# Attention and mixture of experts on one core: expert 5's first layer in pairs of chunks, its list work kept out of the pairs, and two PSUM banks for the last lists

## The chip, the cores and the metric

One core of a Trainium2 chip runs the whole program. The metric is device time in microseconds (us), lower is better. The time of the kernel before is the median of three runs.

## The reference, cut to what matters

An attention over channels makes a 256-wide row for each of 20224 tokens. A gate then assigns each token to one of 8 experts, at most 2528 tokens each, greedily by logit; expert e computes `relu(x @ w1[e]) @ w2[e]` for its tokens.

```
for e in range(8):                       # w1[e]: 256 x 1024, w2[e]: 1024 x 256
    mask = assigned == e
    h = np.maximum(x[mask] @ w1[e], 0.0)
    out[mask] = h @ w2[e]
```

## The kernel before, in words

The attention comes first and takes about the first third of the span. The rest is the experts, numbered p = 0 to 7 in the order in which they are processed. An expert has 2528 rows in 20 columns of 128 (the last has 96), worked on in five chunks of four columns: chunk (p, c) is 512 rows, the last 480.

Every float32 operand is split into a high and a low part, and three products (high by high, low by high, high by low) are summed. So **layer1** takes, for each of 8 blocks of 128 hidden columns, two halves of the contraction by three products: 6 matmuls of 512 columns, 48 for a chunk. TensorE writes `ph` tiles (four PSUM banks, ring of 4); ScalarE writes `hH` (relu, line 1581), VectorE the rest `hL` (line 1586). **layer2** takes 24 matmuls of 256 columns for each of 20 columns into `py` (two banks); ScalarE copies out `y` (line 1628), and GpSimd scatters it to its tokens (line 1630).

For the experts in `PARTED` the chunks (1, 2) and (3, 4) go through **layers** instead: a two-by-two block product with seven products for eight (a Winograd form), over halves of the contraction and halves of the hidden columns, and over the two chunks. For four groups the seven products of three matmuls are issued in the order written out in `STEPS`: 84 matmuls of 512 columns for a pair. It needs sums of weight quarters (**sums_w**, lines 1328 to 1335, spread over the end of the expert before) and of the rows (**turn_parts**, lines 1437 to 1446), and the results are joined with VectorE and ScalarE (lines 1666 to 1686). For an expert outside `PARTED` weights are split by **split_w** (line 1298) and rows by **turn** (lines 1509 to 1516). An expert in `PARTED` loads its second weight into the same buffer as its first, so it asks for it only at the end of the expert before (`load_w`, `LOAD_AT`).

Which tokens an expert gets is found beside the experts' own matmuls, as streams of small steps. **route(p)** searches a threshold (VectorE and ScalarE count, a tiny matmul adds over partitions); **compact(p)** makes the list: a running count, then 20 tests of 128 list places, three to a group. A group is three matmuls into `pi` (line 1022), three ScalarE sign passes with an accumulator (line 1079) and one copy `ext` (line 1082); then some fifteen small VectorE steps. In the kernel before all groups of lists 1 to 7 use one bank, so a group's matmuls follow the copy of the group before.

The order of all engines' instructions is fixed when the program is built, by the class **Order**: it keeps a modelled TensorE time `pe` and VectorE time `dve`; `tick` adds a matmul's time and calls `hook`, which issues whatever is due, the main work (splits, sums, `hL`) ahead of the streams at equal time. A step "P" of a stream goes to TensorE only when its input should have been ready for `margin` (700 ns); "p" goes at once; "A" is a ScalarE step. `want` holds a load back until its list is done.

```
elif eng in "Pp":
    if eng == "p" or st.ready + self.margin <= self.pe:
        self.pe += cost
        st.mine = st.ready = self.pe + PE_TO_DVE
```

Rows of a chunk are gathered by GpSimd (line 1392) and moved twice by SP's queue. `turn(5, 0)` asks for chunk (5, 2); `turn_parts(p, c)` for an even c asks for the two chunks behind it.

Of the kernel before, what the change touches and what calls it, by code (L numbers as in the profile page):

```python
# [8 lines left out]
F32 = mybir.dt.float32  # L9
# [12 lines left out]
E, F = 8, 1024  # L22
# [7 lines left out]
NCOL = -(-CAP // 128)  # L30
LASTC = CAP - (NCOL - 1) * 128
GW = C + E
RB = 3
# [55 lines left out]
SLACK = 450  # L89
DEPTH = 4  # L90
PAD_X = 88
PARTED = (6, 7)
LOAD_AT = (1, 0)
STEPS = (
# [8 lines left out]
def attention_moe(ctx: ExitStack, tc: tile.TileContext, q, k, vt, tau, wg, w1t, w2t, tabs, out):  # L103
# [3 lines left out]
    P = nc.gpsimd  # L107
# [884 lines left out]
    def compact(p):  # L992
# [27 lines left out]
        def tested(pi, g0, n):  # L1020
            for i in range(n):
                PE.matmul(pi[:, i * W:(i + 1) * W], lhsT=G[:, (g0 + i) * 128:(g0 + i + 1) * 128], rhs=E_,  # L1022
                          start=True, stop=True)
# [40 lines left out]
        if p == 0:  # L1064
# [3 lines left out]
                yield "W", 0  # L1068
            yield ve(NCOL)
            V.tensor_scalar(at[:, 0:NACT], sgn[:, 0:NACT], 0.5, COLS / 2.0, op0=OP.mult, op1=OP.add)  # L1070
        for g0 in range(0, NCOL if p else 0, RB):
            n = min(RB, NCOL - g0)
            pi = ps_c.tile([128, 512], F32, name="pi")
            yield "P", n * 75
            tested(pi, g0, n)
            for i in range(n):
                yield "A", 600
                junk = rtile("junk", dt=BF, bufs=2)
                S.activation(junk, pi[:, i * W:i * W + COLS], AF.Sign, bias=rhalf[:, g0 + i:g0 + i + 1], scale=-1.0,
                             accum_out=sgn[:, g0 + i:g0 + i + 1])  # L1080
            yield "A", 200
            S.activation(ext[:, g0:g0 + n], pi[:, 0:n * W].rearrange("p (i w) -> p i w", w=W)[:, :, COLS:W], AF.Copy)
        if p:
            yield ve(NCOL)
            V.tensor_scalar(at, sgn, 0.5, COLS / 2.0, op0=OP.mult, op1=OP.add)
# [59 lines left out]
    class Order:  # L1145
        def __init__(self):
            self.pe = self.dve = 0.0
            self.margin = 0
            self.patient = False
            self.main = []  # L1150
            self.streams = []

# [18 lines left out]
        def hook(self):  # L1171
            moved = True
            while moved:
                moved = False
                best = None
                if self.main:
                    best = (max(self.dve, self.main[0][0]) + self.patient * GAP, 0, None)
                for st in list(self.streams):
                    if st.next is None:
                        self.streams.remove(st)  # L1180
                        continue
                    eng, cost = st.next
                    if eng == "W":
                        st.step()
                        if st.next is None or st.next[0] != "W":
                            moved = True
                            break
                    elif eng == "M":
                        st.mine = max(st.mine, cost)
                        st.step()  # L1190
                        moved = True
                        break
                    elif eng == "A":
                        if st.ready <= self.pe:
                            st.mine = st.ready = self.pe + cost + ACT_LAT
                            st.step()
                            moved = True
                            break
# [4 lines that stand above are left out]
                            st.step()  # L1203
                            moved = True
                            break
                    else:
                        c = (max(self.dve, st.mine) if eng == "V" else self.dve, st.prio(), st)
                        if self.patient and c[1] == EARLY_PRIO:
                            c = (c[0] + EARLY_GAP,) + c[1:]
                        if best is None or c[:2] < best[:2]:  # L1210
                            best = c
                if moved:
                    continue
                if best is not None and best[0] <= self.pe + SLACK:
                    moved = True
                    if best[2] is None:
                        self.run_main()
                    else:
                        st = best[2]
                        self.dve = best[0] + st.next[1]  # L1220
                        st.mine = self.dve + DVE_TO_DVE
                        st.ready = self.dve + DVE_TO_PE
                        st.step()
            plan()
# [12 lines left out]
    o = Order()  # L1237
# [163 lines left out]
    def gather():  # L1401
        for _ in range(2 if queue and queue[0][1] == 0 else 1):
            if queue:
                queue.pop(0)[2]()
# [234 lines left out]
    def layers(p, c):  # L1639
        o.flush(turned[0])  # L1640
        w = parts_w[p]
        (aH, aL), (bH, bL) = xts[p, c], xts[p, c + 1]
        sH, sL = own["s"]
        x = {"11": (aH[:, 0], aL[:, 0]), "12": (aH[:, 1], aL[:, 1]), "s3": (bH[:, 0], bL[:, 0]),
             "22": (bH[:, 1], bL[:, 1])}
        for i, name in enumerate(("s1", "s2", "s4")):
            x[name] = sH[:, i], sL[:, i]
        while queue:
            gather()
        h = [[ffx.tile([128, 8, 512], F32R, name=name) for name in ("hH", "hL")] for _ in range(2)]  # L1650
        seeded = [(ph_tile(), len(phs) - 1) for _ in range(4)]
        fresh = [ps_2.tile([128, 512], F32, name="py") for _ in range(2)]
        sums = {}
        kept = {}

        def product(dst, a, b, g, first=False):
            n = 0
            f = slice(g * 128, (g + 1) * 128)
            for i, l in ((0, 0), (0, 1), (1, 0)):
                PE.matmul(dst, lhsT=w[b][l][:, f], rhs=x[a][i], start=(first and n == 0), stop=(n == 2),  # L1660
                          skip_group_check=True)
                n += 1
                o.tick(227)

        def copy(dst, src):
            S.activation(dst, src, AF.Copy)

        def joined(key, dst, src):
            V.tensor_tensor(dst, src, kept["p7"], op=OP.add)
            sums[key] = dst  # L1670
            o.dve += 690

        for step in STEPS:
            op, g = step.split(".")
            g = int(g)
            A, D = fresh[g % 2], fresh[1 - g % 2]
            Bk, Z = seeded[g % 2][0], seeded[2 + g % 2][0]
            if op[0] in "hl":
                place = {"11": (0, g, A), "12": (0, 4 + g, Z), "21": (1, g, sums.get(("21", g))),
                         "22": (1, 4 + g, sums.get(("22", g)))}  # L1680
                t, f, src = place[op[2:]]
                hH, hL = h[t]
                if op[0] == "h":
                    S.activation(hH[:, f], src, AF.Relu)
                else:
                    V.scalar_tensor_tensor(hL[:, f], src, 0.0, hH[:, f].bitcast(F32), op0=OP.max, op1=OP.subtract)
                    o.dve += 690
            elif op == "cAB":
                copy(Bk, A)
            elif op == "cBZ":  # L1690
                copy(Z, Bk)
            elif op == "p7":
                kept["p7"] = ffx.tile([128, 512], F32, name="p7", bufs=1)
                copy(kept["p7"], D)
            elif op == "j22":
                sums["22", g] = ffx.tile([128, 512], F32, name="c22", bufs=1)
                joined(("22", g), sums["22", g], Z)
            elif op == "j21":
                joined(("21", g), Bk, Bk)
            else:  # L1700
                {"P1": lambda: product(A, "11", "11", g, True), "P7": lambda: product(D, "s3", "t3", g, True),
                 "P6": lambda: product(Bk, "s2", "t2", g), "P2": lambda: product(A, "12", "21", g),
                 "P5": lambda: product(Z, "s1", "t1", g), "P4": lambda: product(Bk, "22", "t4", g),
                 "P3": lambda: product(Z, "s4", "22", g)}[op]()
                settle()
                gather()
        unit[0] += 1
        for _, at in seeded:
            phs[at] = unit[0]
        lows[p, c] = lows[p, c + 1] = unit[0]  # L1710
        return h
# [207 lines left out]
```

## Time and profile before

| what | value |
|---|---|
| median of 3 runs | 1247.6 us (1247.07 to 1250.76) |
| profiled execution | 1246.64 us, of which the span is 1244.6 us |
| granted TensorE clock | 1.0 of full speed throughout |
| TensorE matmul busy | 1228.4 us, 99% of the span |
| VectorE, ScalarE, GpSimd busy | 902.8, 630.9, 386.5 us |

The span is the time from the first to the last instruction of the profiled execution; the execution has 2.04 us around it. Matmul records overlap, so the busy time of TensorE is an upper view of its work; its start times show the pace.

### The profile page before, as it was taken

What the parts mean: (1) busy time and instruction counts of PE and PEld (TensorE: products, weight loads), DVE (VectorE), ACT (ScalarE), POOL (GpSimd) and SP (SyncE); (2) the same over time, 40 slices, a digit from 0 to 9 for tenths busy, and PEclk for the clock granted to TensorE, in tenths of its full rate; (3) what the DMA queues carried; (4) which work ended last, traced back from release to release, by engine and by line L of the source; (5) the groups of instructions that cost most, each with busy time, mean ns of one, the idle gap of its engine ahead of it and who ended that gap; (6) DMA issues with size and microseconds to landing.
All of it is one profiled execution on the core that took longest, in us unless ns stands there. A gap on an engine that the chain in (4) does not pass through costs nothing.

```text
span 1244.6 us, 23776 instructions
## 1 busy us (share of the span) xinstructions
PE 1228.4 (99%) x8734; PEld 1100.3 (88%) x8734; DVE 902.8 (73%) x2574; ACT 630.9 (51%) x1491; POOL 386.5 (31%) x693
## 2 busy tenths in 40 slices
PE   8999999999999999999999999999999999999998
PEld 7888977899888988998999899988988998989898
DVE  6688587798778777867867888887775455756752
ACT  6646653367233543524533655547555544554652
POOL 1000000001442263244443443541453344344422
PEclk9999999999999999999999999999999999999999
DMA  9999876236233054255432633362544335554510
GB/s 314 314 405 415 327 241 217 119 155 236 69 85 104 33 124 134 53 131 117 140 81 73 176 93 99 79 171 55 128 120 105 80 88 148 114 119 114 116 37 33
DMA packets 222516, 179.37 MB, mean 144 GB/s; under 512 B 152384, under 2 KB 193216, under 8 KB 217792
## 3 DMA queue, kind: packets, MB, share of 16 engines
q1 hardware_dynamic: 195328, 98.41, 29.0%
q0 software_dynamic: 17664, 58.22, 14.6%
q10 hardware_dynamic: 9408, 21.24, 4.4%
q8 instruction: 68, 1.11, 0.4%
q14 instruction: 48, 0.39, 0.1%
HBM read 118.06 MB, written 59.77 MB: 143 GB/s over the span
## 4 chain that ended last, share of the span: by engine, by line
PE 81%; issue 7%; DVE 4%; DMA 3%; POOL 3%; ACT 2%; SPq 0%; POOLq 0%; ACTq 0%; DVEq 0%
PE py L1623 30%; PE ph L1578 27%; PE px L285 8%; PE s L337 7%; DMA x_d<-xs 2%; PE pc L811 2%; POOL out_dram L1630 2%; PE ph L1660 2%; PE py L1660 1%; PE px L459 1%; PE pi L1022 1%; DVE acc_q L351 1%; POOL xg L1392 1%; DMA ua<-in_q_dram 1%; DVE acc_k L351 1%
## 5 line engine op out<-in xcount | busy, mean ns | idle before, releaser
L1623 PE MATMUL py<-uc,hH 128*128 128x256 f32 (+1 forms) x2560 | 336.8, 280 | 0.4 <-ACT c L1628 0.3
L1623 PEld LDWEIGHTS py<-uc,hH 128*128 128x128 f32 (+1 forms) x2560 | 314.1, 187 | 2.9 <-ACT c L1628 0.5
L1578 PE MATMUL ph<-xH,ua 128*128 128x512 f32 (+3 forms) x1056 | 285.0, 387 | 0.1
L1586 DVE SCALAR_TENSOR_TENSOR hL<-ph,hH 128x512 fp32r<-128x512 f32 (+3 forms) x264 | 175.6, 666 | 83.1 <-ACT hH L1581 79.9
L1581 ACT ACTIVATE hH<-ph 128x512 fp32r<-128x512 f32 (+3 forms) x264 | 152.7, 579 | 155.9 <-PE ph L1578 149.6
L1578 PEld LDWEIGHTS ph<-xH,ua 128*128 128x128 f32 x1056 | 189.9, 188 | 33.9 <-ACT xH L1542 0.4
L1630 POOL DMA_INDIRECT out_dram<-y,idx x104 | 107.5, 1034 | 325.0 <-ACT y L1628 297.7
L1623 PE MATMUL py<-uc,hL 128*128 128x256 f32 (+1 forms) x1280 | 179.3, 280 | 0.0
L1392 POOL DMA_INDIRECT xg<-x_d,src x156 | 156.2, 1001 | 67.0 <-issue 56.0
L1578 PE MATMUL ph<-xL,ua 128*128 128x512 f32 (+3 forms) x528 | 161.5, 385 | 0.0
L1623 PEld LDWEIGHTS py<-uc,hL 128*128 128x128 f32 (+1 forms) x1280 | 161.0, 187 | 0.2
L1628 ACT ACTIVATE y<-py 128x256 f32<-128x256 f32 (+1 forms) x104 | 39.7, 381 | 151.6 <-PE py L1623 137.9
L1578 PEld LDWEIGHTS ph<-xL,ua 128*128 128x128 f32 x528 | 97.3, 188 | 17.8
L337 PE MATMUL s<-ua 128*128 128x256 f32 x320 | 73.7, 387 | 2.0 <-DMA ua<-in_k_dram 1.5
L288 ACT ACTIVATE xs<-px 128x512 f32<-128x512 f32 (+2 forms) x98 | 49.7, 519 | 47.2 <-PE px L285 45.4
L337 PEld LDWEIGHTS s<-ua 128*128 128x128 f32 x320 | 61.1, 194 | 13.5 <-issue 3.0
L337 PE MATMUL s<-uc 128*128 128x256 f32 x320 | 71.3, 380 | 0.0
L337 PEld LDWEIGHTS s<-uc 128*128 128x128 f32 x320 | 60.3, 190 | 8.8 <-issue 0.8
L285 PE MATMUL px<-aH,vh 128*128 128x256 f32 (+1 forms) x232 | 67.8, 294 | 0.3 <-ACT vh L261 0.3
L285 PE MATMUL px<-aH,vl 128*128 128x256 f32 (+1 forms) x232 | 65.9, 284 | 1.5 <-DVE vl L264 1.5
L1630 POOL DMA_INDIRECT out_dram<-c,idx x30 | 29.4, 981 | 120.4 <-ACT c L1628 109.9
L285 PE MATMUL px<-aL,vh 128*128 128x256 f32 (+1 forms) x232 | 65.9, 285 | 0.0
(432 smaller groups left out, 1977.5 us busy)
## 6 DMA issues: line engine op xcount, KB each, us to landing
x_d<-xs ACTq DMA_DIRECT2D x39, 512.0 KB, 2.7
xr<-xg SPq DMA_DIRECT2D x34, 512.0 KB, 3.3
xq<-xr SPq DMA_DIRECT2D x136, 128.0 KB, 3.7
vr<-in_vt_dram SPq DMA_DIRECT2D x14, 1024.0 KB, 9.9
uc<-in_k_dram SPq DMA_DIRECT2D x18, 512.0 KB, 6.3
uc<-in_q_dram SPq DMA_DIRECT2D x18, 512.0 KB, 8.2
ua<-in_k_dram SPq DMA_DIRECT2D x17, 512.0 KB, 6.5
ua<-in_q_dram SPq DMA_DIRECT2D x17, 512.0 KB, 7.8
```

Source lines behind the costliest of these rows:

```text
L285: mm = PE.matmul(px[:, i * C:i * C + width], lhsT=l_, rhs=a_, start=(j == 0), stop=(j == len(terms) - 1))
L288: S.activation(xs[:, t % TH:t % TH + n, 0:width], px[:, 0:n * width].rearrange("p (t c) -> p t c", t=n), AF.Copy)
L337: newest[0] = PE.matmul(sb[:, ib * C:(ib + 1) * C], lhsT=kt[:, t, ib * 128:(ib + 1) * 128], rhs=qt[:, t, :], start=(first and t == 0 and i ...
L351: V.tensor_tensor(acc, acc, sq, op=OP.add)
L1392: P.indirect_dma_start(out=xg[:n, i, :], out_offset=None, in_=x_d, in_offset=bass.IndirectOffsetOnAxis(ap=at, axis=0))
L1578: PE.matmul(ph[:, 0:nt], lhsT=l[:, w], rhs=x_[:, kb, 0:nt], start=(i == 0), stop=(i == 5))
L1581: S.activation(hH[:, fb, 0:nt], ph[:, 0:nt], AF.Relu)
L1586: V.scalar_tensor_tensor(hL[:, fb, 0:nt], ph[:, 0:nt], 0.0, hH[:, fb, 0:nt].bitcast(F32), op0=OP.max, op1=OP.subtract)
L1623: PE.matmul(py[:n, 0:C], lhsT=l[:, fb, tk], rhs=w[:, d], start=(j == 0), stop=(j == 23))
L1628: S.activation(y[:n], py[:n, 0:C], AF.Copy)
L1630: sd = P.indirect_dma_start(out=out, out_offset=bass.IndirectOffsetOnAxis(ap=idx[:n, col:col + 1], axis=0), in_=y[:n], in_offset=None)
L1660: PE.matmul(dst, lhsT=w[b][l][:, f], rhs=x[a][i], start=(first and n == 0), stop=(n == 2), skip_group_check=True)
```

## The change

`PARTED` becomes (5, 6, 7): the two chunk pairs of expert 5 go through `layers`, with everything that belongs to it (sums of weights at the end of expert 4, sums of rows, the late load of the second weight). While the products of a pair are issued, the streams rest (`o.held`). For the lists of experts 6 and 7 the groups of tests alternate between the bank `pi` and the bank `pc`, and a group's matmuls are issued as "p", after the second sign pass of the group before it, in place of "P" after that group's copy.

```diff
-PARTED = (6, 7)
+PARTED = (5, 6, 7)
...
-        for g0 in range(0, NCOL if p else 0, RB):
-            n = min(RB, NCOL - g0)
-            pi = ps_c.tile([128, 512], F32, name="pi")
-            yield "P", n * 75
-            tested(pi, g0, n)
+        banks = 2 if p >= E - 2 else 1
+
+        def counted(g0, n, kind):
+            pool, name = (pcnt, "pc") if banks == 2 and g0 // RB % 2 else (ps_c, "pi")
+            pi = pool.tile([128, 512], F32, name=name)
+            yield kind, n * 75
+            tested(pi, g0, n)
+            held.append((pi, g0, n))
+        held = []
+        groups = [(g0, min(RB, NCOL - g0)) for g0 in range(0, NCOL if p else 0, RB)]
+        for g in groups[:1 if p else 0]:
+            yield from counted(*g, "P")
+        for at_ in range(len(groups)):
+            pi, g0, n = held.pop(0)
             for i in range(n):
                 yield "A", 600
...
+                if banks == 2 and at_ + 1 < len(groups) and i == min(1, n - 1):
+                    yield from counted(*groups[at_ + 1], "p")
             yield "A", 200
...
+            if banks == 1 and at_ + 1 < len(groups):
+                yield from counted(*groups[at_ + 1], "P")
...
-                for st in list(self.streams):
+                for st in () if self.held else list(self.streams):
...
+        o.held = True
         for step in STEPS:
...
+        o.held = False
```

## Rows read from the trace of the kernel before

**Rows 1.** The page, part 1: busy time of each engine over the span.
```profile
PE 1228.4 (99%) x8734; PEld 1100.3 (88%) x8734; DVE 902.8 (73%) x2574; ACT 630.9 (51%) x1491; POOL 386.5 (31%) x693
```

**Rows 2.** Stretches of experts 5, 6, 7: length, PE, PEld, DVE, ACT, POOL busy, clock.
```profile
916.22:1029.45 113.23, 113.23 (x766) 101.65 (x765) 58.23 (x126) 58.69 (x175) 45.71 (x84) 1.00 0.43 103
1029.45:1135.30 105.85, 105.44 (x699) 95.28 (x697) 68.33 (x110) 57.38 (x112) 46.89 (x86) 1.00 0.52 129
1135.30:1240.20 104.90, 104.83 (x698) 94.90 (x696) 56.61 (x91) 52.18 (x101) 32.33 (x61) 1.00 0.28 69
```

**Rows 3.** Timeline of TensorE, layer 1 of expert 5: start us, us, operation.
```profile
919.15 1.07 PE L1578 MATMUL ph<-xH,ua 128*128 128x512 f32 x4
920.51 0.38 PE L1022 MATMUL pi<-E__106,G 128*128 128x162 bf16 x3
922.15 1.07 PE L1578 MATMUL ph<-xH,ua 128*128 128x512 f32 x4
...
948.35 0.31 PE L1022 MATMUL pi<-E__106,G 128*128 128x162 bf16 x2
```

**Rows 4.** Timeline of TensorE: a 480-row chunk's ends, a pair's ends.
```profile
997.28 1.03 PE L1578 MATMUL ph<-xH,ua 128*128 128x480 f32 x4
1007.67 1.08 PE L1623 MATMUL py<-uc,hH 128*128 128x256 f32 x8
...
1052.12 0.64 PE L1660 MATMUL py<-xH,ua 128*128 128x512 f32 x2
...
1071.49 0.64 PE L1623 MATMUL py<-uc,hH 128*128 128x256 f32 x4
```

**Rows 5.** VectorE's groups by line in expert 6: count, busy us, mean ns, idle before.
```profile
L1443 DVE TENSOR_TENSOR xg<-xg 128x512 f32<-128x512 f32 x8 | 5.5, 692 | 0.3
```

**Rows 6.** Stretches around the starts of expert 5 and expert 6, columns likewise.
```profile
904.00:916.00 12.00, 12.00 (x107) 11.96 (x106) 10.45 (x37) 3.49 (x8) 5.71 (x12) 1.00 0.17 59
916.00:928.00 12.00, 12.00 (x61) 9.49 (x60) 9.93 (x22) 8.69 (x25) 9.03 (x17) 1.00 0.47 134
928.00:940.00 12.00, 12.00 (x62) 9.54 (x61) 5.57 (x9) 8.07 (x27) 0.00 (x0) 1.00 0.81 196
1040.00:1052.00 12.00, 11.74 (x99) 11.34 (x97) 10.24 (x16) 5.23 (x11) 4.46 (x7) 1.00 0.48 133
```

**Rows 7.** Timelines of GpSimd, ScalarE, VectorE, TensorE, start of expert 6.
```profile
1028.66 0.95 POOL L1286 DMA_INDIRECT ub<-in_w2t_dram,ei  x1 [0.30 <-issue]
...
1035.62 0.63 ACT L1295 ACTIVATE uc<-ub 128x512 fp32r<-128x512 f32 x1 [2.59 <-DMA ub<-in_w2t_dram,ei]
...
1036.89 0.68 DVE L1586 SCALAR_TENSOR_TENSOR hL<-ph,hH 128x512 fp32r<-128x512 f32 x1
...
1043.36 1.31 DVE L1437 STREAM_TRANSPOSE xg<-xq 128x512 f32<-128x512 f32 x2 [0.24 <-issue]
...
1048.94 0.69 DVE L1443 TENSOR_TENSOR xL<-xg,xH 128x512 fp32r<-128x512 f32 x1
...
1037.67 1.15 PE L1578 MATMUL ph<-xH,ua 128*128 128x512 f32 x4
...
1049.29 1.18 PE L1623 MATMUL py<-uc,hH 128*128 128x256 f32 x8 [0.26 <-ACT c L1628]
```

**Rows 8.** Timeline of VectorE: list 6, from its head to its index.
```profile
915.32 0.16 DVE L998 CAST cb<-sc_a 128x1 bf16<-128x1 f32 x1
...
954.19 0.17 DVE L1128 SCALAR_TENSOR_TENSOR idx<-bt,src 128x20 int32<-128x20 f32 x1
```

**Rows 9.** ScalarE's groups by line in expert 5, and TensorE's wait in list 5.
```profile
L1079 ACT ACTIVATE junk<-pi,rhalf 128x160 bf16<-128x160 f32 x40 | 15.4, 391 | 3.3 <-PE pi L1022 3.0
L1079 ACT ACTIVATION_READ_ACCUMULATOR junk<-pi,rhalf 128x1 f32 x40 | 8.1, 203 | 0.0
L1082 ACT ACTIVATE ext<-pi 128x6 f32<-128x6 f32 (+1 forms) x14 | 2.5, 178 | 0.0
...
842.92 0.37 PE L1022 MATMUL pi<-E__106,G 128*128 128x162 bf16 x3 [1.42 <-ACT ext L1082]
```

More of the change, by code (lines that the diff above doesn't have):

```diff
@@ L1149, in __init__ @@
             self.patient = False
+            self.held = False
             self.main = []
```

## The prediction, made before the changed kernel ran

> **What bounds the kernel now.** I read the page first, then the stretches of the last experts, then TensorE's timeline inside them, and last the other engines where work is added. The page shows TensorE's matmuls busy for 99% of the span, VectorE for 73%, ScalarE for 51% [rows 1]. Overlapping records make the 99% an upper view, so I checked the timeline: in expert 5 matmuls follow each other at a steady pace with no idle time in the stretch, at clock 1.00 [rows 2]. What counts here is therefore the number of matmuls, and any wait that a late VectorE or ScalarE forces on TensorE. Expert 5 takes 113.23 us, expert 6, which has its pairs already, 105.85, and expert 7 104.90 [rows 2]. The second step is to see how much of the difference is pairs and how much is list work, because both lists 6 and 7 are made inside expert 5.
>
> **List work on TensorE.** Six matmuls of a block take 920.51 − 919.15 = 1.36 us; with a group of list tests ahead of them 922.15 − 920.51 = 1.64 [rows 3]. A group costs 0.28 us. Lists 6 and 7 have 14 groups, and each list a head of two small matmuls that I price alike: 16 × 0.28 = 4.5 us. They are still 14 groups after the change, so this cost moves but does not shrink.
>
> **The pairs, what they save.** I price it three ways.
> - Count: three 512-row chunks of 8 × 1.36 = 10.88 us and one 480-row chunk of 1007.67 − 997.28 = 10.39 [rows 3, 4] make 43.03. Two pairs of 1071.49 − 1052.12 = 19.37 [rows 4] make 38.74. Saved: 4.29 us.
> - Expert 5 without list work, 113.23 − 4.5 = 108.73, against expert 6's 105.85 [rows 2]: 2.9.
> - The same against expert 7's 104.90 [rows 2]: 3.8.
>
> The second holds expert 6's own small waits and the third has no next expert to prepare, so the gross gain lies between 2.9 and 4.3. I take 3.7.
>
> A pair has 12 matmuls fewer than two chunks, at 1.36 / 6 = 0.227 us each [rows 3]. The Trainium skill, "TensorE: Matmul & The Clock Gate", section "Back-to-back issue gap", gives about 131 ns for a sustained 512-column matmul beside its weight load. By it the 24 matmuls saved would be worth an estimated 3.1 us; the trace's pace in this kernel is 0.227, and I go by that.
>
> **What the pairs add on VectorE, and where.** The weight sums at the end of expert 4 are 11 VectorE instructions (seven low parts, four differences) where `split_w` had 4: seven more. The turn of chunk (5, 2) has four mixed sums and three more low parts: seven more again. At 0.69 us [rows 5] each lot is 4.8 us. The joins inside the pairs have room: those of expert 6 fit, and the streams rest there. The two lots fall between 896 and 940 us, in expert 4's last stage and expert 5's first. There VectorE is busy 10.45, 9.93 and 5.57 of three times 12 us [rows 6], so 10.05 us are idle and 9.6 are to be added, while threshold 6 is still being finished: list 6 has its head at 915.32 [rows 8]. Main work goes first at equal time, so what is late first is the list: I expect its head 3 to 6 us later, its first tests at about 925 to 930.
>
> **The wait at expert 5's start.** The start of expert 6 shows what a first expert in pairs does without list work. The second weight's load is issued at 1028.66, behind the four gathers of the next chunk; ScalarE waits 2.59 us for it with the relu copies queued behind, VectorE's low part for the third block comes at 1036.89, TensorE's seventh block needs it at 1037.67 and is a trace slower, the row sums start only at 1043.36, and a `py` bank comes free 0.26 us late at 1049.29 [rows 7]. There was no slack to speak of, and no list. In the changed kernel the same transition comes at 916, with the same load position (`LOAD_AT` is chosen by expert 4, which is not paired), and 3 to 5 us of threshold and list instructions stand in VectorE's order between its low parts. VectorE cannot pass them while it waits behind ScalarE. Bounds: if they all run in time that VectorE idles anyway the extra wait is nothing; if all 9.6 us of added work end up late, 3.2 us of it are still covered (the low part that expert 6's second product reads was done at 1048.94 + 0.69 = 1049.6 [rows 7], and that product comes three matmuls after 1052.12 [rows 4], at 1052.8), and 6.4 us reach TensorE. The nearest row is the start of expert 6, whose 0.26 us lies near the low end; I take a quarter of the way up, 1.7.
>
> **The streams at rest.** List 6 in the kernel before goes from 915.32 to 954.19 [rows 8], groups 4.64 us apart (948.35 − 920.51 over 6) [rows 3]. In the changed kernel the first pair stands at about 916 + 11 + 11 = 938 and rests the streams for 19.4 us; the second pair stands at about 979. List 6 is wanted by `turn_parts(5, 4)` at about 968, and its gathers run beside the products of the second pair. List 7 has the whole of expert 6. So the rest costs nothing as long as list 6 ends by about 979; the price beyond is the third rival. Below nothing I see no gain: in experts 6 and 7 no stream runs in the pairs before either.
>
> **Two banks.** A group needs 3 × (391 + 203) + 178 ns = 1.96 us of ScalarE [rows 9], so 4.64 us a group was not ScalarE's limit. By the planner's own costs (3 × 720 + 320 ns, rounded up to its ticks) I estimate 3.2 us a group, 7 × 3.2 = 22 us for a list. That is what lets list 6 end before 979: two or three groups by 938, the rest from 957 to about 973, some 3 us of small steps. A group's matmuls now wait for a copy two groups back, which the order issues about 1.3 us ahead of them, as far as before. Such a wait did reach TensorE once, 1.42 us in list 5 when ScalarE was behind [rows 9]. Bounds are nothing and one such wait for each list, 2.8; I take 0, since ScalarE is below 75% in these stretches [rows 6].
>
> **The sum.** 3.7 − 1.7 = 2.0 us less than the profiled execution's 1246.64: 1244.6. That execution lies 0.96 below the median of the runs shown, 1247.6, so I forecast 1245.6.
>
> **Rivals.**
> - No new wait: the transition hides as it does for expert 6. Gain 3.7 to 4.3, time 1243.3 to 1243.9. For it: TensorE lost only 0.4 us in all of expert 6 [rows 2]. Against it: that start was at its limit without a list. Chance 0.20.
> - VectorE is the bound between 896 and 940. The 10.05 us idle [rows 6] are mostly waits for ScalarE's copies, and can be filled only in part. If half can be used, 9.6 − 5.0 = 4.6 us are late; if none, 9.6, less the 3.2 covered, and some 1.5 at the end of expert 5's first chunk. TensorE waits 3 to 8 us, the time is 1247 to 1252. It decides against the change from a wait of 3.7 us up. Chance 0.17.
> - List 6 misses the second pair, and rests there until about 998. Its last steps and the gathers of chunk (6, 0) then come 20 us later, with 10 to 15 us to landing and turn (1028.4 to 1043.36 for the same chain [rows 7]); expert 6 would wait up to 5 us on top of 1.7: 1246 to 1251. Chance 0.08.
> - Gathers held up by VectorE. The changed turns and sums read two SBUF operands where the old ones read PSUM, and if such an instruction kept GpSimd out of SBUF, four gathers might each be 0.69 us late [rows 5], the rows of (5, 2) 2.8 us: 1248.4. GpSimd's instructions say no: 46.89 / 86 = 0.545 us each in expert 6, 45.71 / 84 = 0.544 in expert 5 [rows 2]. Chance 0.03. The Trainium skill, "SBUF — State Buffer", section "Who interferes with whom", has this rule for GpSimd instructions that read SBUF; the trace does not bear it out for the time of GpSimd's instructions here.
>
> **How the numbers follow.** The forecast, a gain of 0.4 to 3.7 us, has 0.52, its own range 1243.9 to 1247.2. The range takes in the first rival and most of the second: from 1242.9 (0.4 below the first rival, as medians differ by about that) to 1249.6; about 0.15 is left out. A change of 0.3%, 3.7 us, is about what a measurement of this kernel can tell from none. Faster by more: nearly all of the first rival, 0.18. Slower by more: a quarter of the second, half of the third and some of the fourth, and what I have not seen, 0.12. Within: 0.70.
>
> **What would show it.** Expert 5 about 111 us long for 113.23, with 168 matmuls in its two pairs and one chunk of 48 left; list groups about 3.2 us apart and none inside a pair; ScalarE waiting 2 to 3 us for the second weight at about 919; idle time of TensorE between 919 and 940, in sum 1 to 3 us, put down to VectorE or ScalarE; expert 6 as long as before. It is wrong if that idle time is over 4 us or nothing, if list 6's index lies behind 979, or if TensorE waits at `pi` or `pc`.

## The result, and the profile after

The changed kernel takes 1258.19 us (median of 4 runs, 1257.49 to 1258.33), the kernel before beside it 1247.34. The ratio over the runs is 1.0083, 95% interval 1.0071 to 1.0095: slower, by 10.85 us between the medians, where 1245.6 and "no change that can be told" had the most chance. The profiled execution took 1257.49 us, 10.85 above that of before as well.

The stretches of experts 5, 6 and 7, cut where layer 1 of each begins, with the columns of [rows 2]:

```profile
916.96:1041.56 124.60, 114.16 (x744) 103.18 (x742) 79.11 (x172) 73.81 (x206) 47.60 (x86) 0.96 0.44 110
1041.56:1146.48 104.92, 104.77 (x698) 94.93 (x697) 69.59 (x117) 57.87 (x112) 44.81 (x82) 1.00 0.48 119
1146.48:1251.05 104.57, 104.57 (x698) 94.79 (x696) 56.39 (x91) 52.25 (x101) 32.73 (x61) 1.00 0.28 69
```

Expert 5 takes 124.60 for 113.23 [rows 2], 11.4 us more, and it holds the loss: it starts only 0.7 us later than before, and experts 6 and 7 are 0.9 and 0.3 shorter. Its 24 matmuls fewer (22 by the records, of which a few can be missing) did not help, for TensorE now stands still for 10.4 of the 124.60, and its clock, 1.00 before, is 0.96. Cut at the two pairs, the same view of expert 5:

```profile
916.96:939.47 22.51, 22.47 (x150) 20.11 (x148) 18.18 (x43) 11.42 (x22) 6.97 (x12) 1.00 0.51 122
939.47:958.92 19.45, 19.45 (x87) 15.74 (x85) 13.74 (x26) 14.46 (x27) 10.98 (x20) 1.00 0.77 201
958.92:989.14 30.22, 25.59 (x213) 25.08 (x212) 16.99 (x49) 15.62 (x64) 7.85 (x14) 0.94 0.21 48
989.14:1008.50 19.36, 19.36 (x86) 15.59 (x85) 12.33 (x19) 14.45 (x27) 9.54 (x18) 1.00 0.58 145
1008.50:1041.56 33.06, 27.28 (x216) 26.66 (x214) 17.86 (x39) 17.85 (x68) 12.26 (x22) 0.90 0.32 86
```

The start of the expert is full (22.47 of 22.51), and so are both pairs. The idle time is in the third and fifth stretch, behind each pair. TensorE's timeline names it:

```profile
963.95 0.59 PE L1022 MATMUL pi<-E__106,G 128*128 128x162 bf16 x3 [4.63 <-DVE G L1013]
...
1016.04 0.59 PE L1022 MATMUL pi<-E__106,G 128*128 128x162 bf16 x3 [4.25 <-DVE G L1013]
...
1024.99 0.37 PE L1022 MATMUL pi<-E__106,G 128*128 128x162 bf16 x3 [1.52 <-ACT ext L1093]
```

These are the first test groups of lists 6 and 7, each waiting for `G`, and one later group of list 7 waiting for the copy of its bank: 10.40 us. VectorE's timeline shows what it does between the first pair's end at 958.92 and `G` (lines of after: 1701 is `hL` in a pair, 1683 a joined sum):

```profile
958.94 0.68 DVE L1701 SCALAR_TENSOR_TENSOR hL<-c,hH 128x512 fp32r<-128x512 f32 x1
959.54 1.28 DVE L1701 SCALAR_TENSOR_TENSOR hL<-ph,hH 128x512 fp32r<-128x512 f32 x2
960.74 0.69 DVE L1683 TENSOR_TENSOR ph<-ph,p 128x512 f32<-128x512 f32 x1
962.09 0.69 DVE L1701 SCALAR_TENSOR_TENSOR hL<-ph,hH 128x512 fp32r<-128x512 f32 x1 [0.66 <-ACT hH L1699]
962.70 0.31 DVE L1010 TENSOR_TENSOR E__106<-pc,sc_a 128x160 bf16<-128x160 f32 x1
...
963.01 0.88 DVE L1013 TENSOR_SCALAR G<-rgrid,first 128x2560 bf16<-128x2560 int16 x1
```

The last products are out at 958.92, but their sum, relu and low parts run until 962.78; only then comes the list's turn (`E__106` and the mask `G`, which the tests read). List 6's first tests stand on TensorE two matmuls behind the pair, and TensorE takes its instructions in order, so layer 2 waits behind them.

At the beginning of this pair the mask was two short steps away. VectorE's timeline there:

```profile
940.78 0.15 DVE L1008 COPY first<-pc 128x1 f32<-128x1 f32 x1
943.40 0.69 DVE L1701 SCALAR_TENSOR_TENSOR hL<-py,hH 128x512 fp32r<-128x512 f32 x1 [2.47 <-ACT hH L1699]
```

With `first` done, only `E__106` and `G` were missing, 1.2 us, and VectorE stood idle for 2.47; the rule that streams rest in a pair held them back to its end. No run let these two steps alone through.

Behind the second pair more than the tail stands ahead of list 7's mask:

```profile
1011.67 0.69 DVE L1701 SCALAR_TENSOR_TENSOR hL<-ph,hH 128x512 fp32r<-128x512 f32 x1 [0.67 <-ACT hH L1699]
...
1012.88 1.29 DVE L1345 TENSOR_TENSOR ua<-ub,ua 128x512 fp32r<-128x512 f32 x2
...
1015.11 0.88 DVE L1013 TENSOR_SCALAR G<-rgrid,first 128x2560 bf16<-128x2560 int16 x1
```

These tests stand 26 matmuls of layer 2 behind the pair, and TensorE stops at 1011.79 (1016.04 − 4.25). VectorE's tail ends at 1012.36, 0.6 us later; then come four weight sums and low parts for expert 6 (lines 1345 and 1349) until 1014.8, and then the list. So of the second wait about 0.6 us is the tail itself, 2.5 the weight work and 1.2 the list's own steps. The granted clock in the stretches that follow the two long waits (the last column but two):

```profile
963.90:966.90 3.00, 2.95 (x15) 2.94 (x15) 1.44 (x3) 1.24 (x6) 0.00 (x0) 0.50 0.03 6
966.90:968.00 1.10, 1.10 (x12) 1.03 (x11) 0.00 (x0) 0.00 (x0) 0.00 (x0) 0.97 0.00 0
1016.00:1019.00 3.00, 2.96 (x15) 2.94 (x15) 1.29 (x2) 1.31 (x7) 0.00 (x0) 0.50 0.00 0
1019.00:1022.60 3.60, 3.60 (x24) 3.53 (x22) 0.00 (x0) 0.75 (x2) 0.09 (x1) 0.64 0.00 0
```

Busy, but at 0.50, the lower level (1.2 GHz): 3.0 × 0.5 twice and 3.6 × 0.36 make 4.3 us of lost work. So 10.4 + 4.3 = 14.7 us lost, 10.85 of them left over: about 3.85 came back, 3.3 of it in expert 5 itself (14.7 − 11.4).

Why all seven groups of list 6 stand behind the pair is told by its head and its index on VectorE, against [rows 8]:

```profile
926.22 0.49 DVE L595 TENSOR_TENSOR_SCAN sc_a<-ones_r,m 128x160 f32<-128x160 f32 x1
...
938.79 0.15 DVE L998 CAST cb<-sc_a 128x1 bf16<-128x1 f32 x1
...
988.13 0.18 DVE L1141 SCALAR_TENSOR_TENSOR idx<-bt,src 128x20 int32<-128x20 f32 x1
```

The head (`cb`) is 23 us later than before, right ahead of the rest, and the index 34 us. The running count `sc_a` that the head reads is made at 926.22, 11.4 us later than before (914.79). For the last 12 us VectorE has main work ahead of the head, busy 11.26 of the 12.10 us between: low parts of hidden rows and weights, and the whole turn of chunk (5, 2).

Measured again later, the kernel before took 1246 to 1247 us in two measurements and 1295 to 1296 us in three, one chip showing both, so below each kernel is set against the kernel before of its own measurement, on the first or the second of these levels.

### The profile page after: what moved, and what is told of

Its sections match the earlier page's. It is cut to its first block, busy times and chain, and to the rows that moved or that the text cites. A ratio compares the mean times of both kernels' runs of the same rounds, so it can differ in the third digit from the quotient of the medians.

```text
span 1255.7 us, 23808 instructions
## 1 busy us (share of the span) xinstructions
PE 1227.1 (98%) x8710; PEld 1100.1 (88%) x8710; DVE 925.9 (74%) x2614; ACT 649.2 (52%) x1525; POOL 389.4 (31%) x693
## 4 chain that ended last, share of the span: by engine, by line
PE 72%; issue 11%; POOL 6%; DMA 6%; DVE 2%; ACT 2%; SPq 0%; POOLq 0%; ACTq 0%; DVEq 0%
PE py L1637 26%; PE ph L1592 23%; PE s L337 8%; PE px L285 7%; POOL out_dram L1644 3%; DMA x_d<-xs 2%; POOL xg L1406 2%; PE pc L811 2%; PE ph L1674 1%; DMA ua<-in_q_dram 1%; PE py L1674 1%; PE px L459 1%; DMA uc<-in_q_dram 1%; PE pi L1022 1%; DMA vr<-in_vt_dram 1%
## 5 line engine op out<-in xcount | busy, mean ns | idle before, releaser
L1637 PE MATMUL py<-uc,hH 128*128 128x256 f32 (+1 forms) x2560 | 340.4, 281 | 0.2 <-ACT y L1642 0.2
L1592 PE MATMUL ph<-xH,ua 128*128 128x512 f32 (+3 forms) x928 | 249.8, 387 | 0.1
L1595 ACT ACTIVATE hH<-ph 128x512 fp32r<-128x512 f32 (+3 forms) x232 | 133.9, 578 | 139.9 <-PE ph L1592 134.8
L1592 PEld LDWEIGHTS ph<-xH,ua 128*128 128x128 f32 x928 | 166.4, 188 | 29.4 <-ACT xH L1556 0.4
L1600 DVE SCALAR_TENSOR_TENSOR hL<-ph,hH 128x512 fp32r<-128x512 f32 (+3 forms) x232 | 153.9, 664 | 43.0 <-ACT hH L1595 39.4
L1637 PE MATMUL py<-uc,hL 128*128 128x256 f32 (+1 forms) x1280 | 183.7, 282 | 0.0
L1592 PE MATMUL ph<-xL,ua 128*128 128x512 f32 (+3 forms) x464 | 141.1, 384 | 0.0
L1592 PEld LDWEIGHTS ph<-xL,ua 128*128 128x128 f32 x464 | 85.5, 188 | 15.8
```

What stands on the lines that cost most here:

```text
L1592: PE.matmul(ph[:, 0:nt], lhsT=l[:, w], rhs=x_[:, kb, 0:nt], start=(i == 0), stop=(i == 5))
L1595: S.activation(hH[:, fb, 0:nt], ph[:, 0:nt], AF.Relu)
L1600: V.scalar_tensor_tensor(hL[:, fb, 0:nt], ph[:, 0:nt], 0.0, hH[:, fb, 0:nt].bitcast(F32), op0=OP.max, op1=OP.subtract)
L1637: PE.matmul(py[:n, 0:C], lhsT=l[:, fb, tk], rhs=w[:, d], start=(j == 0), stop=(j == 23))
```

## Experiments

The theories. **A**: VectorE's tail behind a pair; the order written in advance adds 0.69 us for each sum and low part, 24 × 0.69 = 16.6 us for a pair of 19.4, and knows nothing of VectorE's waits for ScalarE, so it takes `G` for done 4 to 5 us too early. **B**: the two banks, by their copies or their issue, cost the time. **C**: it is the rest, which heaps a list right behind a pair, at whatever place. **D** and **E** were formed on the way.

| kernel | us, where the kernel before takes 1246.4 to 1246.8 (first level) | us, where it takes 1295.3 to 1296.3 (second level) |
|---|---|---|
| changed, again | 1257.89, ratio 1.0091 [1.0070, 1.0111] | 1319.42, ratio 1.0175 [1.0134, 1.0215] |
| one bank | | 1328.75 (one run) |
| pairs alone (one bank, no rest) | 1250.01, ratio 1.0026 [1.0013, 1.0039] | |
| banks and rest, no pairs in expert 5 | 1246.24, ratio 0.9998 [0.9987, 1.0008] | |
| no rest | | 1312.92, 1313.57, 1310.79 |
| extra matmuls ahead of the tests | | 1314.68, 1319.60, 1315.11 |
| 2 us behind a pair | 1261.86, ratio 1.0123 [1.0106, 1.0139] | 1316.31, ratio 1.0153 [1.0131, 1.0175] |
| the same, list 6's end free in a pair | 1245.74, ratio 0.9995 [0.9984, 1.0007] | 1305.57, 1305.40, ratios 1.0068 [1.0043, 1.0093], 1.0062 [1.0041, 1.0083] |
| the same with 2.5 us | 1244.74, ratio 0.9984 [0.9973, 0.9995] | |

**The changed kernel again**, as a yardstick for the others, once on each level:

> The changed kernel itself, unaltered, as the yardstick for the others on the same chip. Each theory is about where its time lies, so each expects the same here: about 10.9 us above the kernel before run beside it (ratio near 1.0087), with TensorE waiting 4 to 5 us for G right behind the first pair and again behind the second pair of expert 5, 1.5 us for a copy of list 7, and a granted clock of 0.50 behind the two long waits. On a chip on which the kernel before takes some 1296 us, as in the first four runs, the distance may be larger: there the pairs' own first products waited for ScalarE.

> The changed kernel unaltered, as the yardstick of this call: ratio to the kernel before 1.0085 to 1.0095 on a chip where that takes 1247 us, with waits for G of 4.6 and 4.3 us. Where it takes 1296 us no run of the changed kernel has been made: 15 to 25 us above the kernel before there, 4 to 5 us of it at the first products of the pairs, which wait there for a copy of ScalarE.

On the first level it is 11.5 us above the kernel before (10.9 in the result above), with the same three waits; on the second 24.1, the upper end of what was expected there.

**Without the second bank, and without the rest.**

```
-        banks = 2 if p >= E - 2 else 1
+        banks = 1
```

> The change with one bank for all lists (a group's matmuls follow the copy of the group before, as before the change); pairs in expert 5 and resting streams stay. Theory A (VectorE's tail): behind a pair VectorE still has joins and low parts to do, the order does not know of them, and a list's first group of tests stands in TensorE's queue before VectorE can have made its mask G. The first group's place does not depend on the banks, so both waits for G, 4.6 and 4.3 us, stay, the 1.5 us wait for a copy goes: 1255 to 1257 us. Theory B (the two banks): groups issued at once are what TensorE waits at; without them the waits vanish and the pairs' gain is left: 1243 to 1246 us. Theory C (the rest): as A.

One run, 1328.75, above the changed kernel's 1319.42 on that level. The first wait for `G` stays, 4.63 us, so B falls as its cause. Two things came otherwise than expected: the second wait for `G` is absent, and one for a copy, 1.5 us in the changed kernel, is 3.41. TensorE's timeline:

```profile
1049.40 0.43 PE L1022 MATMUL pi<-E__106,G 128*128 128x162 bf16 x2 [3.41 <-ACT ext L1093]
```

This is the last group of list 6, behind the second pair. With one bank its groups are 4.7 us apart, the list misses the pair, and its index comes at 1059.2 instead of 1027.1 in the changed kernel on that level. So the second bank has no part in the wait for `G`, but lets list 6 end ahead of the second pair.

```
-        o.held = True
```

> The change without the rest: streams go on inside the pairs' products; pairs in expert 5 and two banks stay. Theory A: G of list 6 then stands near the start of the pair, ahead of most joins, so no wait of 4 us for G; but ScalarE, busy 14.5 of 19.4 us in a pair, would take some 10 us of list passes more, and TensorE waits for copies of the lists or of the pairs instead: 1248 to 1256 us. Theory C (the rest alone costs the time, since it puts a list's first steps right behind a pair): no waits over 1 us, 1243 to 1246 us.

> The changed kernel without the rest during a pair; two banks stay. Theory A and D: list 6 runs through the pair as in the kernel before, no wait for G over 1 us, its indices are out before 985; the total is near that of the pairs alone with one bank (ratio 1.0026 to the kernel before), a little lower since two banks give a list at 3 us a group: 1246 to 1250. Rival E: waits for ScalarE's copies and VectorE's sums inside the pairs, 6 us or more in all, total at 1254 or above.

> The changed kernel without the rest during a pair, two banks kept. Theory D: no wait for G over 1 us, list 6's indices before 985, total 1246 to 1250 on a chip where the kernel before takes 1247. Rival E: 6 us or more of waits for ScalarE's copies and VectorE's sums inside the pairs, total 1254 or above. Where the kernel before takes 1296: 1313, as measured there.

All three fell on the second level, where they do not decide between the theories. No wait for `G`, and 5.8 to 8.6 us less than the changed kernel by the three kernels' times (1310.79 against 1319.42 measured side by side), but other waits in place of it: 3.2 to 3.9 us inside the second pair for a sum (`c`, L1683), and 2.4 to 2.9 at the end of expert 5's layer 2 for a copy.

**The two halves of the change apart.** First both edits above together, pairs in expert 5 alone:

> Pairs in expert 5 alone: one bank, and lists run on through a pair's products, as in the kernel before. Theory A: no rest, so no tests heaped right behind a pair; no wait for G over 1 us; list tests of about 4.3 us a group of copies lie inside the pair, where each third test group may hold VectorE and ScalarE up for 1 to 2 us; total from before - 3.9 (pairs' gain undiminished) to before + 2. Theory B: the same, as the second bank is gone too. Theory C (the rest itself): the same. It tells what the pairs alone are worth: if this is 10 us above before as well, the pairs are the cause and all three theories fall.

1250.01, 3.6 us above the kernel before. The stretch of expert 5, and TensorE's waits for list copies in it (us in total, times, longest):

```profile
917.58:1035.32 117.74, 113.13 (x743) 99.71 (x742) 79.42 (x177) 73.27 (x206) 47.59 (x84) 0.99 0.46 116
```

```profile
PE pi L1022 <- ACT ext L1093: 2.8, 2, 2.3
```

There is no wait for `G`, as A and C have it, but the gain is gone too: 4.6 us of 117.74 are idle, 2.8 by list copies and most of the others by four waits of 0.4 us inside the pairs for ScalarE. The upper end of the expectation, + 2, was passed. With a list running through them the pairs cost 3.6 us more than they save; some arrangement of the list is needed. Then the rest and the banks without pairs in expert 5:

```
-PARTED = (5, 6, 7)
+PARTED = (6, 7)
```

> Expert 5's layer 1 in ordinary order as before; the rest during pairs (experts 6 and 7, which carry no list) and the two banks stay. Theory A: no pair of expert 5, so no tail; no wait for G over 1 us, total before +- 1.5 us (lists at 3 us a group instead of 4.3 us). Theory B: if the two banks' copies or their issue cost, the total is 3 to 10 us above before here as well. Theory C: as A.

```profile
916.63:1029.48 112.85, 112.85 (x766) 101.25 (x765) 58.59 (x126) 58.19 (x175) 45.87 (x84) 1.00 0.43 104
```

1246.24, the same as before, and expert 5 without idle time. The two banks cost nothing by themselves, nor gain (the rest has no list to hold here, so this kernel says nothing of it): a list in 27 us instead of 39 (974.10 − 947.26 between the indices of lists 6 and 7, against 993.25 − 954.19) was not what TensorE waited for.

**VectorE's tail made known to the order.**

```
         o.held = False
+        o.dve = max(o.dve, o.pe + 2000)
```

> The change, with one line more behind a pair's products: the order's VectorE time is set to at least its TensorE time plus 2.0 us, so that list steps and tests are placed later; the same work. Theory A: both waits for G go and with them the stretches at half clock behind them (4.6 + 4.3 us idle, 3 to 4 us of clock): 1244 to 1248 us, expert 5 about 110 to 113 us. Theory B: the groups issued at once still wait: within 2 us of 1258. Theory C: the list is still right behind the pair, so at least half of the loss stays: 1252 or more.

> The same kernel as the run with 2 us added to VectorE's reckoned time behind a pair. Theory A (VectorE's tail behind the pair is later than the order reckons, and the first tests meet it): the waits for G go, 8.9 us and the 4.3 us of low clock with them, and on a chip like that of the first profile it lands at after - 12 = about 1245 to 1247, from 0.3% below before to equal. Theory B (the two banks' copies and issue cost): the copies of both lists are still there, 1.5 us goes at most, so about 1256. Theory C (any list packed between the pairs of expert 5 costs what the rest saves, wherever it starts): the wait changes its name (VectorE's hL or ScalarE's xH) and the total stays at 1252 to 1258.

The first fell on the second level (1316.31, a wait of 0.5 us for `G` and one of 5.6 for `xH` at the start of expert 6; the changed kernel took 1319.42 on that level). The second, on the first level, gave 1261.86: 4 us slower still than the changed kernel, above even what C had expected (1252 to 1258), and with C's sign, a wait that changes its name. TensorE's timeline:

```profile
964.17 0.38 PE L1022 MATMUL pi<-E__106,G 128*128 128x162 bf16 x3 [0.53 <-DVE G L1013]
...
1039.61 2.24 PE L1592 MATMUL ph<-xH,ua 128*128 128x512 f32 x4 [10.16 <-ACT xH L1527]
```

A's wait is gone, 8.9 us down to 0.5, and in its place expert 6 cannot start for 10.16 us. VectorE's timeline gives the chain:

```profile
1014.26 0.17 DVE L1098 TENSOR_SCALAR at<-sgn 128x20 int32<-128x20 f32 x1
...
1017.99 0.18 DVE L1141 SCALAR_TENSOR_TENSOR idx<-bt,src 128x20 int32<-128x20 f32 x1
...
1038.19 1.32 DVE L1523 STREAM_TRANSPOSE ph<-xq 128x512 f32<-128x512 f32 x2 [18.82 <-DMA xq<-xr]
```

List 6's tests were out before the second pair, but its index arithmetic fell into the pair and rested there until 1014; the index came at 1018 instead of 988. GpSimd's first gather of expert 6's rows, in the changed kernel and then in this one:

```profile
991.28 0.99 POOL L1406 DMA_INDIRECT xg<-x_d,src  x1 [0.22 <-issue]
```

```profile
1017.75 0.98 POOL L1406 DMA_INDIRECT xg<-x_d,src  x1 [0.22 <-DVE bt L1138]
```

The gather is 26.5 us later; the rows are transposed at 1038.19, when they have landed, and TensorE had nothing more to do from 1029.45 (1039.61 − 10.16). And behind the wait the clock again (stretches of the same kernel):

```profile
1030.00:1039.60 9.60, 0.00 (x0) 0.00 (x0) 1.33 (x3) 0.78 (x4) 7.66 (x15) 0.56 0.97 199
1039.60:1042.60 3.00, 2.99 (x7) 2.21 (x8) 1.27 (x2) 0.99 (x4) 0.00 (x0) 0.50 0.70 205
1042.60:1045.60 3.00, 3.00 (x12) 2.16 (x11) 0.69 (x1) 1.50 (x6) 0.00 (x0) 0.62 0.85 134
```

This is theory **D**: two mechanisms, the tail behind the pair, and the rest that holds up a list nearly done. The changed kernel escaped the second because its order, which took `G` for done too early, had placed the whole list earlier: 58 matmuls of layer 2 stand between list 6's last tests and the second pair there, 22 here, and the index arithmetic no longer comes ahead of the pair. **E** is C sharpened: the pairs leave VectorE and ScalarE too little room, so the time returns under any order.

**The list's end free.** As above, and the stream of a list whose tests are all issued is not held:

```
-        o.add(compact(p), ...)
+        o.add(compact(p), ...).of = routed[p]
...
         for at_ in range(len(groups)):
+            r["loose"] = at_ + 1 == len(groups)
...
-                for st in () if self.held else list(self.streams):
+                for st in [s for s in self.streams if not self.held
+                           or getattr(s, "of", {}).get("loose")]:
```

> The kernel with 2 us added behind a pair, with one thing more: when the last tests of a list are out, its last copies and its index arithmetic on VectorE may run inside a pair's products; all other streams rest as before. Theory D, formed from the run before it (the wait behind the pairs is VectorE's tail, but taking it away put list 6's index arithmetic behind the second pair, and the gathered rows of expert 6 came 10.2 us late): list 6's indices are out about 30 us earlier, near 988 instead of 1018, the wait for xH at the start of expert 6 falls below 1 us, and the total lies 12 to 13 us below the 1261.9 of that run, 1246 to 1250. Rival E (the pairs of expert 5 leave VectorE and ScalarE too little room, so that the time comes back under any order): the index arithmetic stops the pair instead, TensorE waits inside the second pair for ph or p by 3 us or more, and the total stays above 1254.

> The kernel with 2 us behind a pair and with list 6's last copies and index arithmetic free to run inside a pair. Theory D (VectorE's tail, and behind it the lateness of list 6's indices): on a chip on which the kernel before takes some 1247 us, list 6's indices near 988, no wait over 1 us for xH at the start of expert 6, no wait for G over 1 us, 12 us below the 1261.9 of the same kernel without this freedom: 1246 to 1250. Rival E (pairs of expert 5 leave VectorE and ScalarE too little room under any order): 3 us or more of waits for ph or p inside the second pair, total above 1254. On a chip on which the kernel before takes some 1296 us: 1302 to 1311, as measured there.

> The kernel with 2 us behind a pair and list 6's last copies and index arithmetic free inside a pair, once more, for a chip on which the kernel before takes some 1247 us. Theory D: list 6's indices near 988, no wait over 1 us for xH at the start of expert 6 or for G, 1246 to 1250. Rival E: waits for ph or p of 3 us or more inside the pairs on this chip too, total above 1254. Where the kernel before takes 1296: 1302 to 1309, as twice measured.

The first two fell on the second level, the third on the first.

On the first level it takes 1245.74, 16 us below the kernel without this freedom and a little below the 1246 to 1250 of D; E had said above 1254. C falls as well on this level: the list still stands right behind the pair, and the loss is gone. VectorE's timeline at the second pair (lines one further):

```profile
985.25 0.18 DVE L1099 TENSOR_SCALAR at<-sgn 128x20 int32<-128x20 f32 x1 [5.55 <-ACT junk L1089]
...
987.58 0.18 DVE L1142 SCALAR_TENSOR_TENSOR idx<-bt,src 128x20 int32<-128x20 f32 x1
988.12 0.69 DVE L1702 SCALAR_TENSOR_TENSOR hL<-py,hH 128x512 fp32r<-128x512 f32 x1 [0.36 <-ACT hH L1700]
```

The arithmetic takes 2.3 us and is done before VectorE has its first low part of the pair. On the second level it was 14.0 us below the changed kernel beside it (1305.40 against 1319.42). With 2.5 us for 2:

> The same with 2.5 us instead of 2. Theory D: the wait of 0.5 us for G behind the first pair and the 0.5 to 0.8 us for cb behind the second go, list 6's indices are out half a microsecond later and still in time for expert 6; total 0 to 1.5 us below the run with 2 us beside it. If list 6's last tests miss the second pair: indices near 1015, a wait of some 10 us at the start of expert 6, total 10 to 13 us above it.

1244.74, the fastest of all, ratio 0.9984 with the whole interval below 1. The head is as late as in the changed kernel, but the first tests of list 6 no longer wait. The head on VectorE, the first tests on TensorE, and the stretches of experts 5 and 6:

```profile
938.95 0.15 DVE L998 CAST cb<-sc_a 128x1 bf16<-128x1 f32 x1
...
964.12 0.38 PE L1022 MATMUL pi<-E__106,G 128*128 128x162 bf16 x3
```

```profile
916.77:1027.31 110.54, 109.52 (x735) 98.52 (x734) 77.91 (x161) 68.08 (x177) 48.86 (x86) 1.00 0.49 125
1027.31:1133.71 106.40, 106.23 (x706) 95.76 (x705) 70.73 (x126) 62.10 (x141) 44.84 (x82) 1.00 0.48 117
```

Expert 5 is 2.7 us shorter than before; part of list 7's tests went into expert 6, which is 0.55 longer.

**The low clock by itself.** Work of no use, overwritten by the tests, keeps TensorE busy ahead of the first group of lists 6 and 7:

```
+            for _ in range(19 if banks == 2 and kind == "P" else 0):
+                warm(pi)
             tested(pi, g0, n)
```

> The change, with 19 matmuls of 512 columns (4.3 us at full clock) of the identity into the list's own bank ahead of the first group of lists 6 and 7; the tests overwrite what they leave. They fill most of the two waits for G and move nothing else. If the half clock behind the waits (0.50 for 3 us each, 0.64 for 3.6 more in list 7) comes from TensorE's idle time, the clock stays 1.00 there and the time falls by 3 to 4.5 us, to 1254 to 1255; the waits' own 9 us stay as dummy work. If the clock has another cause, the time stays within 1 us of 1258 or rises.

> The changed kernel with 19 matmuls of no use (512 columns, their result overwritten by the tests) ahead of the first test group of lists 6 and 7, so that TensorE has 4.3 us of work while VectorE finishes behind the pair. Nothing of the result changes. Theory A with the clock: the two waits of 4.6 and 4.3 us for G fall below 1 us, the time itself is spent on the extra matmuls, and only the low clock behind the waits is saved: granted clock 1.00 in the stretches after both pairs, total 3.5 to 5 us below the changed kernel run before (1257.9), 1253 to 1254.5. Rival (the low clock has another cause than the wait, VectorE's or ScalarE's load for one): the clock is 0.50 there all the same, and the total stays at 1257 or above.

> The changed kernel with 19 matmuls of no use (512 columns, overwritten by the tests) ahead of the first test group of lists 6 and 7. If the low clock behind the two waits for G comes of TensorE's standing still: clock 1.00 in the stretches after both pairs, total 3.5 to 5 us below the changed kernel in the same call. If it has another cause: 0.50 there all the same, total within 1 us of it.

All three fell on the second level; the last was measured side by side with the changed kernel: 1315.11 against 1319.42, 4.3 us. The clock behind the pairs in the changed kernel, and then with the extra matmuls:

```profile
1001.70:1004.70 3.00, 2.96 (x15) 2.94 (x15) 1.43 (x3) 1.24 (x6) 0.00 (x0) 0.50 0.02 5
1058.25:1061.25 3.00, 2.96 (x16) 2.87 (x17) 1.29 (x2) 1.31 (x7) 0.00 (x0) 0.54 0.00 0
```

```profile
1002.40:1005.40 3.00, 2.94 (x27) 2.91 (x28) 1.45 (x4) 1.23 (x6) 0.00 (x0) 1.00 0.00 0
1056.65:1059.65 3.00, 3.00 (x28) 2.92 (x28) 1.29 (x2) 1.32 (x7) 0.00 (x0) 1.00 0.02 5
```

The same kind of work, 15 matmuls in 3 us at 0.50 and 27 at 1.00; in the other two runs with extra matmuls the clock behind both pairs is 1.00 as well. That standing still lowers the clock is shown; the size is less firm, for the same kernel took 1319.60 in another measurement.

## Why the prediction was wrong

- **The pairs' gain.** Right: 3.7 (2.9 to 4.3) was said, 3.85 comes out of the changed kernel's balance, 3.3 within expert 5. In the kernel with 2.5 us, TensorE's busy time in experts 5 and 6 together is 109.52 + 106.23 = 215.75 for 218.67 [rows 2]: 2.9, the lower bound.
- **The wait at expert 5's start.** Said 1.7, measured 0.04 in 22.5 us. The work of weights and turns fitted; VectorE was busy 18.18 of these 22.51. What gave way was the list.
- **List 6's head 3 to 6 us later, first tests at 925 to 930.** It came 23 us later. The prediction counted VectorE's idle time, 10.05 us from 904 to 940, as room for the 9.6 added. VectorE between 896 and 940, before and then after:

```profile
896.00:940.00 44.00, 44.00 (x293) 38.99 (x292) 31.23 (x90) 24.35 (x72) 18.07 (x33) 1.00 0.50 124
896.00:940.00 44.00, 43.61 (x326) 40.89 (x326) 35.88 (x96) 21.88 (x47) 18.00 (x31) 1.00 0.45 106
```

It still idled for 8.1 of the 44 us while the head waited its turn. So "two or three groups by 938" became none, and the whole list stood behind the first pair. This step failed first, but by itself it costs nothing: in the kernel with 2.5 us the head is as late (938.95).
- **"So the rest costs nothing as long as list 6 ends by about 979."** This is the step that failed. It looked for the price at the list's deadline, where gathered rows might be late. The price stood at the list's beginning: list 6, starting behind a pair, starts behind VectorE's tail of 3.9 us (958.92 to 962.78), with `G` 0.9 us more; list 7 behind a tail and 2.5 us of weight work. The prediction had "the joins inside the pairs have room" from expert 6; they have, but no list waits behind the pairs there, so the tail never showed. In the sum the rest stood at nothing; it cost 8.9 us of waits.
- **List 6 misses the second pair.** This rival, with 0.08 and a price up to 5 us, was near: the index came at 988.13, the second pair began at 989.14. Where it did happen, with 2 us behind a pair, it cost a wait of 10.16 us and low clock besides: the mechanism was right, the price half of the true one. It happened with one bank too.
- **Two banks.** The pace, 3.2 us a group by estimate, was (982.36 − 966.98) / 5 = 3.1 by TensorE's timeline. One copy wait of 1.5 came, inside the bound of 2.8 where 0 was taken. The two banks alone change nothing (1246.24), but with pairs in expert 5 one bank is too slow for list 6.
- **The clock.** Missing from the sum and from the bounds: 4.3 us, as much as one of the waits that brought it.

The signs named in advance came: idle time of nothing between 919 and 940, list 6's index behind 979, TensorE waiting at `pi`. That other causes add nothing on the first level is shown by the mended order, which keeps the pairs, the banks and the rest but for a list's end, and stands at 0.9984 of the kernel before. Where list 6's head loses its 23 us is seen on VectorE (11.4 by 926, 12 behind main work); not shown is why the order left it there, and whether an earlier head would give more.

## What to carry to other kernels

When work is barred from a stretch, price both ends of the bar: what was running when it fell (a list with only its arithmetic to do cost 10 us for 2.3 us of work), and what starts first when it lifts, on the engine that is then furthest behind. In an order written in advance for an engine that works in order, the one instruction put too early stops everything behind it; its model must know the tail of the slower engine, and 0.5 us of it still showed. A mend that removes a wait is only judged by the total: the next wait here was larger.

## What was not expected of the hardware

- TensorE stood still for 4.63 and 4.25 us, and both times the granted clock was 0.50 for the next 3 us; behind the wait of 1.52 us it was 1.00 (1025 to 1028). The Trainium skill, "TensorE: Matmul & The Clock Gate", section "What's actually happening", says that the throttled state is the default and that activity releases it; the two stretches agree, and so do the runs in which extra matmuls kept the clock at 1.00.
- The kernel before had two levels, 1246.4 to 1246.8 us and 1295.3 to 1296.3. On the second, the changed kernel's TensorE waits in the middle of five of its six pairs for a copy by ScalarE, for which the profile gives no releaser on the chip (timelines of TensorE and ScalarE):

```profile
986.85 1.22 PE L1674 MATMUL ph<-sH,ub 128*128 128x512 f32 x2 [4.32 <-ACT ph L1680]
```

```profile
986.22 0.58 ACT L1680 ACTIVATE ph<-py 128x512 f32<-128x512 f32 x1 [4.61 <-remote]
```

At 3 to 4.3 us a pair it takes about twice what a pair gains (3.7 / 2 = 1.9). The mended order stays 9.5 and 10.1 us behind the kernel before on that level (ratios 1.0068 and 1.0062), more than two such pairs account for. What makes the level, and the rest of that distance, was not found.
